# An attention and mixture-of-experts kernel: another set-up of the routing, the last head's low parts on VectorE, and the sum of query halves one head earlier

## The chip, the cores and the metric

The kernel runs on one core of a Trainium2 chip. The metric is the time of one execution on the device in microseconds (us): the median of several runs, lower is better.

## The reference

Attention with queries averaged in pairs, then a mixture of experts in which each token goes to the one expert with the largest logit.

```python
q_pool = q.reshape(B, H, S // 2, 2, D).mean(axis=3)          # B, H, S, D = 4, 8, 1152, 64
scores = 1 / np.sqrt(D) * np.matmul(q_pool, k.transpose(0, 1, 3, 2))
attn = np.exp(scores - scores.max(-1, keepdims=True))
attn = attn / (attn.sum(-1, keepdims=True) + 1e-09)
x = np.matmul(attn, v).transpose(0, 2, 1, 3).reshape(B * S // 2, H * D)   # 2304 x 512
xn = x / (np.linalg.norm(x, axis=-1, keepdims=True) + 1e-06)
en = expert_emb / (np.linalg.norm(expert_emb, axis=-1, keepdims=True) + 1e-06)
logits = xn @ en.T / tau                                     # 8 experts
expert_idx = np.argmax(logits, axis=1)
gate_w = softmax(logits)[np.arange(N), expert_idx]
out[mask] = gate_w[mask, None] * (np.maximum(x[mask] @ w1[e], 0.0) @ w2[e])   # per expert e
```

Everything is in float32; the kernel keeps the accuracy by splitting float32 values into a high and a low 16-bit part.

## The kernel before

**Attention.** There are 32 heads, written here as head 0 to head 31 (`g` in the code); two heads make a pair, four pairs a batch. The loop over `g` (line 1071 on) writes nine steps for each head, `c` = 0 to 8, one for each 128 keys. A step holds, in the order of the letters in `ORDER`: S, the scores of 128 keys by 576 queries on TensorE (line 309) and their exponential on ScalarE (line 311); M, matmuls for the row maxima of the next head (lines 260 and 266, then ScalarE 272 and VectorE 275, 277, 283); E, the low part of the exponentials of one step earlier, `EL = e - high(e)` (line 313); P, the product of the exponentials of the head before with the values (lines 389 to 391), which reads the low parts in line 391; X, everything else that a table puts at that step. Every engine runs its own instructions in the order in which this loop writes them.

The low part of a step is on GpSimd for the steps listed in `POOL_EL` (1, 2, 4, 5, 6, 7 in an even head, 0, 1, 3, 5, 8 in an odd one) and on VectorE for the others. `PVH` sets what P takes: in step 0 keys 0 to 3 of the first query tile, in step 1 keys 4 to 7, in step 2 key 8, then the other tiles. So TensorE comes to the low part of step 7 at the end of step 1 of the next head.

**Preparation of a pair.** `load_qk` reads queries and keys by the SP queue at step 2 of an even head (`LPOS`). `prep` gives seven operations that `QPOS` puts into the odd head that follows: `qsum`, the sum of the two query halves (GpSimd, line 174), at step 1, then high and low parts of keys and queries (ScalarE 177 and 186, GpSimd 180 and 189). The DMAs that move the parts are in the next even head.

**Set-up of the routing.** `setup_routing` (line 435) normalises the expert vectors: squares and their sum, a square root by three Newton iterations (`root_steps`), a reciprocal, high and low parts, two DMA transposes. It returns a list of steps, and from head 4 on the loop takes one after each step `c`.

**Routing of a batch.** `rsteps` splits the attention output, makes logits, and `chains` finds the expert and the rank of each token: `mx`, `lgs`, `mark`, `mk`, `choose` (one-hot `oh`), `rank` (matmuls), `rk`, `rq`, `rm`, and `oneh`, a comparison of 128 x 512 or 128 x 640 elements into `AV` (line 614). For batches 0 to 2 these run beside the attention of the next batch, also one step of the list after each step `c`; some are on GpSimd (`w`), some on VectorE.

**The end of attention.** In heads 30 and 31 the output of the last batch is split in three quarters of its columns (`split`, lines 485 to 494): high part on ScalarE, low part on VectorE (488), DMAs, and the sum of squares on VectorE (494). Iteration `g` = 32 holds only the P of head 31. Then the string `TAIL` gives the order in which normalising of head 31 (`N`, `J`), the last quarter (`c`, `R`), logits (`A`, `L`), expert choice, gathers and the first expert blocks are written, and `run` the other blocks: gather of 128 tokens (867), transpose (871), `mm1` (911), `relu` (917, 918), `mm2` (928), scaling (934), scatter (935). The expert weights are read as float32 and split by ScalarE (884) and VectorE (882).

Of the kernel before, what the change touches and what calls it, by code (L numbers as in the profile page):

```python
# [10 lines left out]
BF16 = mybir.dt.bfloat16  # L11
# [31 lines left out]
def attn_moe(ctx: ExitStack, tc: tile.TileContext, qt, kt, vt, emb, tau, w1, w2, out):  # L43
# [259 lines left out]
    def sc(g, c):  # L303
# [8 lines left out]
        eng = nc.gpsimd if c in (POOL_EL[g % 2] if g else POOL_E0) else nc.vector  # L312
# [18 lines left out]
    QPOS = [1, 2, 3, 3, 5, 7, 8]  # L331
# [12 lines left out]
    TAIL = 'x.0.0 x.0.1 A.0 A.1 A.2 A.3 mm1.0.0 j.4 N c.1.5.0 j.4 c.1.5.1 J c.0.1.0 j.2 c.0.1.1 R x.0.2 x.0.3 ch.1.2 ch.1.3 cl.1.0 cl.1.1 cl.1.2 cl.1.3 x.1.0 x.1.1 x.1.2 x.1.3 S A.4 mm1.0.1 mm1.1.0.0.6 L mm1.1.0.6.12 q.5 relu.0.0 q.2 mm1.1.1.0.4 q.5 mm1.1.1.4.12 mm2.0.0.6 q.11 relu.0.1 E relu.1.0 relu.1.1 g.24 gather.2 gather.3 gather.4 gather.5 xtr.2 xtr.3 xtr.4 regl.5 regl.6 wl.5.0 wl.5.1 mm2.0.6.24 mm2.1 mm1.2.0 g.2 mm1.2.1 fin.0 fin.1 cst.5.0.0 cst.5.0.1'  # L344
# [90 lines left out]
    def setup_routing():  # L435
# [23 lines left out]
        def turn():  # L459
# [24 lines left out]
    def split(T, x, xh, c0, c1, now, xt):  # L484
# [35 lines left out]
    def last_part(b):  # L520
# [715 lines left out]
```

## Time and profile before

| | |
|---|---|
| Time, median of 3 runs (lowest, highest) | 681.13 us (678.55, 682.29) |
| The profiled execution: its own time, its span | 676.58 us, 674.9 us |
| Busy share of TensorE, VectorE, ScalarE, GpSimd | 93%, 83%, 75%, 63% |
| Granted TensorE clock, mean | 0.99 |

The profile gives one execution on the chip. A share of busy time is a mean over stages: attention up to about 439 us and expert blocks after it. Below, a head is the stretch from its first exponential on ScalarE (line 311, nine in each head) to that of the next head. A `[... <-X]` behind a row is the idle time of that engine just before the instruction, and what ended it.

### The profile page before, as it was taken

Reading aid. Unit: us, or ns where it says so; the run is one execution under the profiler, and the core shown is the slowest. Engines: PE = TensorE matmul, PEld = TensorE weight load, DVE = VectorE, ACT = ScalarE, POOL = GpSimd, SP = SyncE. Lnnn points to the kernel's source line nnn. Section 1 sums busy time; section 2 is a strip of 40 time slices with the busy share of each in tenths; the row PEclk is TensorE's granted clock in tenths of the full one; section 3 lists DMA queues with packets and bytes.
Section 4 is the critical chain, followed back from the end, with each engine's and each line's share of the span. In section 5 each row is a group of like instructions: output and inputs, shape, how many; then the busy total and the mean of one; then the engine's idle time right before and its main releaser. Section 6 shows DMA issues by size and latency. Waiting matters only on the chain. (4 is left out here: it accounts for less than half of the span.)

```text
span 674.9 us, 22284 instructions
## 1 busy us (share of the span) xinstructions
PE 628.4 (93%) x8898; PEld 471.3 (70%) x8918; DVE 563.2 (83%) x983; ACT 509.4 (75%) x839; POOL 425.2 (63%) x349
## 2 busy tenths in 40 slices
PE   8999979999899799899899989799999999999994
PEld 2477757777678577678677768686776767768671
DVE  6778777888787978887878898996758999999996
ACT  2888767788887688897789867532548898988985
POOL 5699899897897887887996858202231233464231
PEclk9999998999999999999999999799999999999999
DMA  6844615537675529675529615996899977232881
GB/s 197 244 120 132 184 39 164 155 95 200 160 146 153 155 67 227 152 168 168 138 77 232 156 56 182 197 284 140 245 287 297 198 207 187 69 85 72 207 189 44
DMA packets 82990, 109.18 MB, mean 162 GB/s; under 512 B 51406, under 2 KB 57070, under 8 KB 82880
## 3 DMA queue, kind: packets, MB, share of 16 engines
q1 hardware_dynamic: 79280, 96.68, 55.7%
q0 software_dynamic: 3600, 11.01, 5.7%
q8 instruction: 72, 1.18, 0.7%
q14 instruction: 38, 0.31, 0.1%
HBM read 118.52 MB, written 10.22 MB: 191 GB/s over the span
## 5 line engine op out<-in xcount | busy, mean ns | idle before, releaser
L313 POOL TENSOR_TENSOR ar<-ar 128x576 f16<-128x576 f32 x175 | 222.4, 1278 | 56.9 <-ACT ar L311 56.2
L311 ACT ACTIVATE ar<-st 128x576 f32<-128x576 f32 x288 | 187.0, 652 | 63.0 <-PE st L309 59.0
L309 PE MATMUL st<-ar 128*128 128x288 f16 (+1 forms) x1152 | 188.6, 286 | 0.4 <-ACT ar L311 0.3
L882 DVE TENSOR_TENSOR ar<-ld,ar 128x1024 bf16<-128x1024 f32 x144 | 167.5, 1218 | 10.0 <-ACT ar L884 9.2
L391 PE MATMUL acc<-ar 128*128 128x65 f16 (+1 forms) x1440 | 166.9, 193 | 6.2 <-DVE ar L313 3.9
L389 PE MATMUL acc<-ar 128*128 128x65 f16 (+1 forms) x1440 | 167.8, 194 | 0.2
L390 PE MATMUL acc<-ar 128*128 128x64 f16 (+1 forms) x1440 | 167.7, 196 | 0.0
L389 PEld LDWEIGHTS <-ar 128*128 128x128 bf16 (+1 forms) x1440 | 136.3, 98 | 32.1 <-issue 19.7
L390 PEld LDWEIGHTS <-ar 128*128 128x128 bf16 (+1 forms) x1440 | 136.0, 98 | 22.9 <-issue 2.0
L884 ACT ACTIVATE ar<-ld 128x1024 f16<-128x1024 f32 x144 | 143.1, 1050 | 8.3 <-DMA ld<-in_w_dram 8.3
L275 DVE CUSTOM_DVE_ANT_0 my<-m,my 128x512 bf16<-128x512 f32 x139 | 95.6, 687 | 57.1 <-PE m L260 38.7
L391 PEld LDWEIGHTS <-ar 128*128 128x128 f16 (+1 forms) x1440 | 136.4, 100 | 8.0 <-DVE ar L313 4.4
L935 POOL DMA_INDIRECT out_dram<-ar,six x21 | 42.1, 2004 | 135.5 <-ACT ar L934 125.2
L313 DVE TENSOR_TENSOR ar<-ar 128x576 f16<-128x576 f32 x113 | 124.0, 1098 | 0.0
L911 PEld LDWEIGHTS <-ar 128*128 128x128 f16 (+1 forms) x2016 | 114.1, 98 | 5.4 <-issue 1.2
L911 PE MATMUL hps<-ar 128*128 128x128 f16 x2016 | 116.5, 219 | 0.9 <-DMA ar<-ar 0.9
L928 PE MATMUL ops<-ar 128*128 128x512 f16 (+1 forms) x484 | 111.2, 379 | 2.3 <-ACT ar L884 1.3
L309 PEld LDWEIGHTS <-ar 128*128 128x128 f16 (+1 forms) x1152 | 95.5, 98 | 21.6 <-issue 3.4
L928 PEld LDWEIGHTS <-ar 128*128 128x128 f16 x504 | 48.4, 98 | 56.2 <-ACT ar L884 1.7
L272 ACT ACTIVATE my<-m 128x512 bf16<-128x512 f32 x139 | 82.8, 595 | 2.4 <-PE m L260 2.3
L260 PE MATMUL m<-ld,qz 128*128 128x512 f16 (+1 forms) x264 | 62.8, 299 | 10.2 <-DVE mc L277 6.1
L260 PE MATMUL m<-kd,qz 128*128 128x512 f16 x132 | 50.2, 380 | 6.6 <-DVE mc L275 3.2
(212 smaller groups left out, 654.9 us busy)
## 6 DMA issues: line engine op xcount, KB each, us to landing
ld<-in_w_dram SPq DMA_DIRECT2D x160, 512.0 KB
ld<-in_q_dram SPq DMA_DIRECT2D x16, 576.0 KB
ld<-in_v_dram SPq DMA_DIRECT2D x16, 576.0 KB
ar<-ld SPq DMA_DIRECT2D x31, 288.0 KB
ld<-in_k_dram SPq DMA_DIRECT2D x15, 576.0 KB
ar<-ld SPq DMA_DIRECT2D x33, 144.0 KB
ar<-qhl SPq DMA_DIRECT2D x32, 144.0 KB
xs<-xh SPq DMA_DIRECT2D x13, 256.0 KB
```

The costliest lines, as they stand in the source:

```text
L260: nc.tensor.matmul(out=o, lhsT=QZ[s][:, c:c + 128], rhs=kr, start=True, stop=True)
L275: nc.vector.tensor_tensor_reduce(out=y, in0=m, in1=y, scale=1.0, scalar=-3e38, op0=ALU.add, op1=ALU.max, accum_out=mc[p, h][:, 1, t:t + 1])
L309: nc.tensor.matmul(out=st[:, a, 0:HQ], lhsT=KK[s][0:n, h, k, c * 128:(c + 1) * 128], rhs=QQ[s][0:n, h, k, a * HQ:(a + 1) * HQ], start=(k = ...
L311: nc.scalar.activation(out=e.rearrange("p (a q) -> p a q", a=2), in_=st[:, :, 0:HQ], func=AF.Exp, scale=1.0 / 16)
L313: return lambda: eng.tensor_tensor(out=EL[g % 2][:, c], in0=e, in1=hi(e), op=ALU.subtract)
L389: nc.tensor.matmul(out=a[r], lhsT=hi(e[:, w]), rhs=VV[s][:, c, h, 0:65], start=(x == 0), stop=False)
L390: nc.tensor.matmul(out=a[r, 0:64], lhsT=hi(e[:, w]), rhs=VV[s][:, c, h, 65:129], start=False, stop=False)
L391: nc.tensor.matmul(out=a[r], lhsT=el[:, w], rhs=VV[s][:, c, h, 0:65], start=False, stop=(x == NC - 1))
L882: nc.vector.tensor_tensor(out=dl.bitcast(BF16), in0=src, in1=dh, op=ALU.subtract)
L884: nc.scalar.activation(out=dh, in_=src, func=AF.Copy)
L911: nc.tensor.matmul(out=hp[j, f][:, t * 128:t * 128 + 128], lhsT=wv(w, i % 2, c)[:, u], rhs=xt[:, 2 * c + i // 2], start=(c == 0 and t == 0 ...
L928: nc.tensor.matmul(out=op[j], lhsT=ht[:, c // 4, i // 2, (c % 4) * 128:(c % 4) * 128 + 128], rhs=wv(w, i % 2, c), start=(k == 0), stop=(k ...
```

## The change

- **Set-up.** The squares of the expert vectors with their sum, the scaling by the reciprocal and the high part move to ScalarE. The product with 64 becomes an operation on the 16 x 1 reciprocal. The list grows from 22 steps to 42 with gaps: the Newton iterations stand in head 6 and not in heads 4 to 6, the rest in heads 6 to 8.
- **Last head.** For `g` = 31 all nine low parts are on VectorE. In `split` the sum of squares on VectorE goes; `first_squares` makes it on ScalarE, at `Q` in `TAIL`.
- **Query halves.** `qsum` for pair p + 2 leaves step 1 of the odd head and is written at step 7 (`QSUM`) of the even head before, the head whose step 2 issues the load that it reads.
- **Routing of a batch.** The lists of `rsteps` have empty steps put in and operations regrouped.

```diff
-        eng = nc.gpsimd if c in (POOL_EL[g % 2] if g else POOL_E0) else nc.vector
+        eng = nc.gpsimd if g < 2 * B * NP - 1 and c in (POOL_EL[g % 2] if g else POOL_E0) else nc.vector
...
-    QPOS = [1, 2, 3, 3, 5, 7, 8]
+    QSUM = 7
+    QPOS = [2, 3, 3, 5, 7, 8]
...
-    TAIL = 'x.0.0 x.0.1 A.0 A.1 A.2 A.3 mm1.0.0 j.4 N c.1.5.0 ...
+    TAIL = 'x.0.0 x.0.1 A.0 A.1 A.2 A.3 mm1.0.0 Q j.4 N c.1.5.0 ...
...
-        steps = [[loads], [masks], [iotas], []]
-        steps += [[f] for f in [
-            lambda: gp.tensor_scalar(out=taub, in0=taub, scalar1=XS * 64.0, scalar2=None, op0=ALU.mult),
-            lambda: gp.tensor_tensor(out=e2, in0=e, in1=e, op=ALU.mult),
-            lambda: v.tensor_reduce(out=sq, in_=e2, axis=AX.X, op=ALU.add),
-        ] + root + [
-            lambda: gp.tensor_scalar(out=r, in0=n, scalar1=1e-6, scalar2=None, op0=ALU.add),
-            lambda: v.reciprocal(out=r, in_=r),
-            lambda: gp.tensor_scalar(out=e2, in0=e, scalar1=r, scalar2=64.0, op0=ALU.mult, op1=ALU.mult),
-            lambda: gp.tensor_copy(out=eh[:, 0], in_=e2),
-            lambda: gp.tensor_tensor(out=eh[:, 1], in0=e2, in1=eh[:, 0], op=ALU.subtract),
-            turn,
-        ]]
+        def squared():
+            nc.scalar.activation(out=e2, in_=e, func=AF.Square, accum_out=sq)
+
+        parts = [
+            (0, loads), (1, masks), (2, iotas), (7, squared), (10, root[0]), (10, root[1]),
+            (30, lambda: gp.tensor_scalar(out=taub, in0=taub, scalar1=XS * 64.0, scalar2=None, op0=ALU.mult)),
+            (25, lambda: gp.tensor_scalar(out=r, in0=n, scalar1=1e-6, scalar2=None, op0=ALU.add)),
+            (28, lambda: v.reciprocal(out=r, in_=r)),
+            (34, lambda: gp.tensor_scalar(out=r, in0=r, scalar1=64.0, scalar2=None, op0=ALU.mult)),
+            (36, lambda: nc.scalar.activation(out=e2, in_=e, func=AF.Copy, scale=r)),
+            (37, lambda: nc.scalar.activation(out=eh[:, 0], in_=e2, func=AF.Copy)),
+            (39, lambda: gp.tensor_tensor(out=eh[:, 1], in0=e2, in1=eh[:, 0], op=ALU.subtract)),
+            (41, turn),
+        ]
+        steps = [[] for _ in range(42)]
+        for i, f in enumerate(root[2:]):
+            steps[18 + i].append(f)
+        for i, f in parts:
+            steps[i].append(f)
...
-        if now:
-            sv = work.tile([128, 384], BF16, tag="sv", name="sv", bufs=1)
-            v.tensor_tensor_reduce(out=sv[:, 0:(c1 - c0) * 128], in0=xc, in1=xc, scale=1.0, scalar=0.0, op0=ALU.mult, op1=ALU.add, accum_out=ssq[:, T:T + 1])
...
+        def first_squares():
+            for i in range(n):
+                nc.scalar.activation(out=sj[:, 128:512], in_=x[:, i, 0:384], func=AF.Square, accum_out=ssq[:, T0 + i:T0 + i + 1])
...
-            return steps + [[f] for f in crit[:5] + cnt + crit[5:] + oneh]
+            return steps + [[f] for f in crit[:3]] + [[], crit[3:4], crit[4:5], [], cnt[0:1], cnt[1:], [], crit[5:6], crit[6:7], crit[7:8], crit[8:10], crit[10:], [], oneh]
...
-                plist[p + 2] = prep(p + 2)
                 for pos, f in zip(QPOS, plist[p + 2][0]):
                     at(pos, f)
             if g % 2 == 0 and p + 2 < NPAIR:
                 at(LPOS, lambda p=p: load_qk(p + 2))
+                at(QSUM, lambda p=p: (plist.update({p + 2: prep(p + 2)}), plist[p + 2][0].pop(0)()))
```

GpSimd's instructions around the Newton iterations (423, 424 before; 424, 425 now), first before, from the end of head 4; `ar` is the exponentials' arena, `ld` the loaded keys.

```order
L313 TENSOR_TENSOR ar<-ar 128x576 x3
L423 TENSOR_TENSOR n_279<-n_278 16x1
L423 TENSOR_TENSOR n_279<-n_279,esq 16x1
L313 TENSOR_TENSOR ar<-ar 128x576
L174 TENSOR_TENSOR qs<-ld 128x576
L424 TENSOR_SCALAR n_279<-n_279 16x1
L424 TENSOR_TENSOR n_278<-n_279,n_278 16x1
L313 TENSOR_TENSOR ar<-ar 128x576
```

And now, from the end of head 4 too:

```order
L313 TENSOR_TENSOR ar<-ar 128x576 x4
L174 TENSOR_TENSOR qs<-ld 128x576
L313 TENSOR_TENSOR ar<-ar 128x576 x3
L180 TENSOR_TENSOR ld<-ld 128x576
L313 TENSOR_TENSOR ar<-ar 128x576 x2
L189 TENSOR_TENSOR qhl<-qs,qhl 128x576
L180 TENSOR_TENSOR ld<-ld 128x576
L313 TENSOR_TENSOR ar<-ar 128x576
L424 TENSOR_TENSOR n_279<-n_278 16x1
L424 TENSOR_TENSOR n_279<-n_279,esq 16x1
```

The first iteration has left head 5, where the operations of `prep` stand, for the start of head 6, and `qs` stands in front of two low parts that it stood behind: step 7 of the even head and step 0 of the odd one.

VectorE in head 16, with the routing of batch 0, before:

```order
L313 TENSOR_TENSOR ar<-ar 128x576
L402 TENSOR_SCALAR r<-acc 128x5
L403 RECIPROCAL r<-r 128x5
L405 TENSOR_TENSOR xx<-acc,r 128x4x64
L407 TENSOR_SCALAR xx<-acc,r 64x64
L614 TENSOR_TENSOR av<-iota,rm 128x512
L275 ISA my,mc<-m,my 128x512
L275 ISA mc 128x1
L224 SCALAR_TENSOR_TENSOR ar<-ld,ar 128x18x64
```

And now:

```order
L403 TENSOR_SCALAR r<-acc 128x5
L404 RECIPROCAL r<-r 128x5
L406 TENSOR_TENSOR xx<-acc,r 128x4x64
L408 TENSOR_SCALAR xx<-acc,r 64x64
L275 ISA my,mc<-m,my 128x512
L275 ISA mc 128x1
L224 SCALAR_TENSOR_TENSOR ar<-ld,ar 128x18x64
L622 TENSOR_TENSOR av<-iota,rm 128x512
L275 ISA my,mc<-m,my 128x512
```

The comparison `av` has gone from in front of a maximum (275) to behind it and behind the values' low part (224).

VectorE in head 31, before (488 is the low half of the split, 494 the squares):

```order
L407 TENSOR_SCALAR xx<-acc,r 64x64
L488 SCALAR_TENSOR_TENSOR xh<-xx,xh 128x3x128
L494 ISA sv,ssq<-xx 128x384
L494 ISA ssq 128x1
L488 SCALAR_TENSOR_TENSOR xh<-xx,xh 128x3x128
L494 ISA sv,ssq<-xx 128x384
L494 ISA ssq 128x1
L313 TENSOR_TENSOR ar<-ar 128x576
L488 SCALAR_TENSOR_TENSOR xh<-xx,xh 128x3x128
```

And now:

```order
L408 TENSOR_SCALAR xx<-acc,r 64x64
L313 TENSOR_TENSOR ar<-ar 128x576
L495 SCALAR_TENSOR_TENSOR xh<-xx,xh 128x3x128
L313 TENSOR_TENSOR ar<-ar 128x576
L495 SCALAR_TENSOR_TENSOR xh<-xx,xh 128x3x128
L313 TENSOR_TENSOR ar<-ar 128x576 x2
L495 SCALAR_TENSOR_TENSOR xh<-xx,xh 128x3x128
L313 TENSOR_TENSOR ar<-ar 128x576 x2
```

The squares are gone from VectorE and five low parts have come in between.

## Rows read from the trace of the kernel before

**Rows 1.** Windows, heads 3 to 6: from:to length, busy us by engine, PEclk, DMA.

```profile
56.16:68.78 12.62, 12.25 (x194) 9.37 (x193) 10.34 (x22) 10.54 (x20) 11.95 (x9) 1.00 0.28 73
68.78:79.93 11.15, 11.15 (x189) 9.02 (x188) 7.83 (x19) 9.31 (x17) 7.86 (x14) 1.00 0.80 220
79.93:94.61 14.68, 12.46 (x194) 9.47 (x193) 12.24 (x25) 10.54 (x19) 14.11 (x21) 1.00 0.17 54
94.61:110.99 16.38, 13.04 (x189) 9.95 (x188) 10.44 (x19) 9.52 (x18) 15.76 (x16) 0.90 0.56 154
```

**Rows 2.** Waits, 79 to 106 us: who waited for whom, total us, times, longest.

```profile
DVE er L470 <- POOL er L469: 3.7, 1, 3.7
...
PE acc L391 <- POOL ar L313: 2.3, 2, 1.7
```

**Rows 3.** Waits of TensorE in heads 15 and 16, 211 to 239 us.

```profile
PE mt L293 <- DVE mc L275: 1.9, 1, 1.9
...
PE m L260 <- DVE mc L275: 1.7, 1, 1.7
```

**Rows 4.** Waits, 425 to 440 us.

```profile
ACT ar L531 <- DVE xx L405: 6.5, 1, 6.5
...
PE acc L391 <- DVE ar L313: 3.9, 4, 2.0
```

**Rows 5.** Windows: a stretch in the P of head 31, columns as in Rows 1.

```profile
429.40:436.23 6.83, 5.27 (x68) 3.86 (x65) 6.69 (x15) 4.06 (x5) 0.00 (x0) 0.50 1.20 204
```

**Rows 6.** Groups on GpSimd: count, then busy us, mean ns, idle before.

```profile
L313 POOL TENSOR_TENSOR ar<-ar 128x576 f16<-128x576 f32 x175 | 222.4, 1278 | 56.9 <-ACT ar L311 56.2
...
L174 POOL TENSOR_TENSOR qs<-ld 128x576 f32<-128x576 f32 x15 | 27.8, 1852 | 2.7 <-DMA ld<-in_q_dram 2.7
...
L423 POOL TENSOR_TENSOR n<-n 16x1 f32<-16x1 f32 x3 | 2.1, 697 | 0.0
...
L423 POOL TENSOR_TENSOR n<-n,esq 16x1 f32<-16x1 f32 x3 | 0.5, 180 | 0.2
```

**Rows 7.** Windows of heads 8 and 12, columns as in Rows 1.

```profile
123.60:135.07 11.47, 11.24 (x189) 9.01 (x188) 9.47 (x18) 9.32 (x17) 8.80 (x8) 1.00 0.76 208
...
173.99:186.08 12.09, 11.33 (x188) 9.02 (x187) 8.50 (x19) 10.24 (x20) 8.76 (x7) 1.00 0.79 184
```

**Rows 8.** Timeline of TensorE in head 9: start, us, then the instruction.

```profile
136.91 0.65 PE L309 MATMUL st<-ar 128*128 128x288 f16 x4
```

**Rows 9.** Timeline: a query load and its sum, then head 8, then a load in head 12.

```profile
10.57 0.58 SPq L137 DMA_DIRECT2D ld<-in_q_dram  x1
...
14.87 1.40 POOL L174 TENSOR_TENSOR qs<-ld 128x576 f32<-128x576 f32 x1 [2.65 <-DMA ld<-in_q_dram]
...
128.72 0.61 SPq L137 DMA_DIRECT2D ld<-in_q_dram  x1
...
131.76 1.15 POOL L313 TENSOR_TENSOR ar<-ar 128x576 f16<-128x576 f32 x1 [0.39 <-ACT ar L311]
...
181.00 0.60 SPq L137 DMA_DIRECT2D ld<-in_q_dram  x1
```

**Rows 10.** Timeline of VectorE in heads 15 and 16: two operations of the routing.

```profile
218.36 0.19 DVE L605 TENSOR_REDUCE mk<-key 128x4 f32<-128x32 f32 x1 [0.80 <-POOL key L587]
...
233.53 1.56 DVE L614 TENSOR_TENSOR av<-iota,rm 128x512 f16<-128x512 f32 x1
```

**Rows 11.** Timeline of VectorE, 419 to 438 us.

```profile
419.69 2.19 DVE L488 SCALAR_TENSOR_TENSOR xh<-xx,xh 128x384 f16<-128x384 f32 x1 [0.59 <-ACT xh L487]
...
422.28 3.14 DVE L488 SCALAR_TENSOR_TENSOR xh<-xx,xh 128x384 f16<-128x384 f32 x1
...
425.82 0.75 DVE L313 TENSOR_TENSOR ar<-ar 128x576 f16<-128x576 f32 x1
...
426.49 1.50 DVE L488 SCALAR_TENSOR_TENSOR xh<-xx,xh 128x384 f16<-128x384 f32 x1
...
429.06 0.54 DVE L488 SCALAR_TENSOR_TENSOR xh<-xx,xh 128x384 f16<-128x384 f32 x1
```

More of the change, by code (lines that the diff above doesn't have):

```diff
@@ L343, in attn_moe @@
     C00 = [18, 19, 20, 21]
-    TAIL = 'x.0.0 x.0.1 A.0 A.1 A.2 A.3 mm1.0.0 j.4 N c.1.5.0 j.4 c.1.5.1 J c.0.1.0 j.2 c.0.1.1 R x.0.2 x.0.3 ch.1.2 ch.1.3 cl.1.0 cl.1.1 cl.1.2 cl.1.3 x.1.0 x.1.1 x.1.2 x.1.3 S A.4 mm1.0.1 mm1.1.0.0.6 L mm1.1.0.6.12 q.5 relu.0.0 q.2 mm1.1.1.0.4 q.5 mm1.1.1.4.12 mm2.0.0.6 q.11 relu.0.1 E relu.1.0 relu.1.1 g.24 gather.2 gather.3 gather.4 gather.5 xtr.2 xtr.3 xtr.4 regl.5 regl.6 wl.5.0 wl.5.1 mm2.0.6.24 mm2.1 mm1.2.0 g.2 mm1.2.1 fin.0 fin.1 cst.5.0.0 cst.5.0.1'
+    TAIL = 'x.0.0 x.0.1 A.0 A.1 A.2 A.3 mm1.0.0 Q j.4 N c.1.5.0 j.4 c.1.5.1 J c.0.1.0 j.2 c.0.1.1 R x.0.2 x.0.3 ch.1.2 ch.1.3 cl.1.0 cl.1.1 cl.1.2 cl.1.3 x.1.0 x.1.1 x.1.2 x.1.3 S A.4 mm1.0.1 mm1.1.0.0.6 L mm1.1.0.6.12 q.5 relu.0.0 q.2 mm1.1.1.0.4 q.5 mm1.1.1.4.12 mm2.0.0.6 q.11 relu.0.1 E relu.1.0 relu.1.1 g.24 gather.2 gather.3 gather.4 gather.5 xtr.2 xtr.3 xtr.4 regl.5 regl.6 wl.5.0 wl.5.1 mm2.0.6.24 mm2.1 mm1.2.0 g.2 mm1.2.1 fin.0 fin.1 cst.5.0.0 cst.5.0.1'
     RC = 1
@@ L547, in logit @@
                 lmm(L[:, i * NE:(i + 1) * NE], xbt, 3, 4, 2 * i, first=False, last=(i == n - 1))
-        return cut, rest, squares, add_up, logit
+        return cut, rest, first_squares, squares, add_up, logit
     def chains(b, last):
@@ L690, in rsteps @@
         if not late_:
-            return steps + [[f] for f in crit[:5] + cnt + crit[5:] + oneh]
+            return steps + [[f] for f in crit[:3]] + [[], crit[3:4], crit[4:5], [], cnt[0:1], cnt[1:], [], crit[5:6], crit[6:7], crit[7:8], crit[8:10], crit[10:], [], oneh]
         sel, pick, nxt = early_steps()
-        steps += [crit[0:2], crit[2:4], [crit[4], cnt[0]], cnt[1:], [], crit[5:6], sel[0:1], crit[6:8], crit[8:10] + sel[1:2], [crit[10], sel[2]]]
-        steps += [sel[3:5], sel[5:7], sel[7:9], oneh, pick[0:2], pick[2:5], pick[5:6], pick[6:7], [], pick[7:8], [], pick[8:10], pick[10:11], pick[11:13], nxt]
+        steps += [crit[0:3], [], crit[3:5], [], cnt, crit[5:6], sel[0:1], crit[6:8], crit[8:10] + sel[1:2], [crit[10], sel[2]]]
+        steps += [sel[3:5], sel[5:7], sel[7:9], pick[0:2], pick[2:5], oneh, pick[5:6], pick[6:7], [], pick[7:8], [], pick[8:10], pick[10:11], pick[11:13], nxt]
         return steps
@@ L1168, in attn_moe @@
         ended.append(True)
-        cut, rest, squares, add_up, logit = last_part(B - 1)
+        cut, rest, first_squares, squares, add_up, logit = last_part(B - 1)
         L = small("L")
@@ L1183, in attn_moe @@
             "R": rest,
-            "S": squares,
+            "S": squares, "Q": first_squares,
             "A": lambda i: fl[i](L),
```

## The prediction

> **What bounds the kernel now.** I read the windows of the heads first, because a mean over 675 us hides which head is long. An even head without routing takes 11.15 us, and TensorE is busy for all of it; an odd one takes 12.62 us, with TensorE busy for 12.25 (head 3 in [rows 1]). So TensorE sets the time where nothing disturbs it, and only waits of TensorE, or its clock, can be won back. Heads 5 and 6, with the set-up, take 14.68 and 16.38 us, 2.06 and 5.23 more than the undisturbed 12.62 and 11.15: 7.3 us together. GpSimd is busy for 14.11 and 15.76 of these [rows 1], nearly without a pause, so there it is the bound. The waits show how that reaches TensorE: it waits for low parts of GpSimd, and VectorE stands 3.7 us at the reciprocal behind GpSimd, with the maxima queued behind it [rows 2]. In heads 15 and 16 TensorE waits 1.9 and 1.7 us for VectorE's maxima [rows 3]. At the end of attention it waits 3.9 us for low parts of VectorE [rows 4], and the granted clock is 0.50 of full, the lower of its two levels (1.2 and 2.4 GHz), for 6.83 us from 429.40 on, where TensorE had just stood waiting [rows 5].
>
> **The sum's base.** The profiled execution has a span of 674.9 us and took 676.58, 4.55 under the median of 681.13. I work the gains out from its rows and take them off the median.
>
> **Set-up.** Three operations of GpSimd on 16 x 512 elements go (squares, scaling, copy). By the nearest row, 1.28 us for a low part of 128 x 576 [rows 6], that is at most 3.8 us; the small operation that comes in costs at most 0.70. The larger part is that the Newton iterations leave head 5, where GpSimd also has keys and queries to split. I follow GpSimd's queue through head 6 as it is now written. Without the set-up head 5 takes 12.6 us, so head 6 begins at 79.93 + 12.6 = 92.5. The last low part of head 5 comes at the earliest 1 us later, 93.5. Then there are 13 small operations in five groups: the first of a group took 0.70, a following one 0.18 [rows 6], with gaps of about 0.1 that makes 5 x 0.70 + 8 x 0.18 + 0.4 = 5.3. Six low parts at 1.15 (128 x 576 undelayed, [rows 9]) are 6.9, the query sum 1.40 [rows 9]. The low part of step 7 is so done at 93.5 + 5.3 + 6.9 + 1.4 = 107.1. TensorE comes to it 1.84 us after the next head begins: in head 9 the third group of scores starts at 136.91, right behind that product, and the head began at 135.07 [rows 7, 8]. Head 7 would begin at 92.5 + 11.15 = 103.65, so TensorE is there at 105.5 and waits 1.6 us. Of 7.3 us there remain about 2 with the wait at the reciprocal: **-5.4**. Bounds: GpSimd at its mean of 1.28 a low part and 1.85 for the sum [rows 6] adds 1.2, and heads 4, 7 and 8 can each lose some 0.5, so -2.5; nothing left, -7.3. What ScalarE takes over is four instructions of under 0.7 us in heads in which it is busy for 9.3 to 10.5 of 11.2 to 12.6 us [rows 1], so they are hidden.
>
> **Query sum.** GpSimd does the same work, earlier. No row shows TensorE waiting for GpSimd in an undisturbed odd head, so nothing is won there. The new order puts the sum in front of the low part of step 7, and in front of both stands the query load. From its issue to the sum it took 14.87 - 10.57 = 4.3 us. In head 8 the load is issued at 128.72, so it is there at 133.0; the low part of step 6 ends at 132.9 [rows 9]. Then the sum to 134.4 or 134.9, the low part to 135.6 or 136.2, and TensorE needs it at 136.9: hidden, with 0.7 to 1.3 us to spare. In head 12, where routing DMAs stand before the load in SP's queue, it is issued at 181.00 [rows 9], 7.0 us after the head's start instead of 5.1 [rows 7]: there at 185.3, sum and low part done at 188.4, while TensorE is there at 186.08 + 1.84 = 187.9. It waits 0.5 us, or 1.5 if the busier queue costs the load 1 us more. Head 20 is of the same kind. I take **+1.3** for the 13 odd heads, between 0 and 4 (a third of a microsecond in each).
>
> **Routing of a batch.** In head 15 VectorE stood 0.80 us for GpSimd's key with a maximum queued behind; in head 16 the comparison `av` of 1.56 us stood before the maximum for which TensorE waited 1.7 [rows 3, 10]. The first now asks after the normalising, some 1.5 us later, when the key is done; the second now stands behind the maximum and the values' low part. That is 0.8 + 1.5 for batch 0. For batch 1, where the same pattern occurs with shorter waits, I count 1.2, for batch 2 nothing: **-3.5**. Bounds: 0, if `av` only delays the next maximum; -7.2, if both waits vanish in both batches.
>
> **Last head.** VectorE loses five sums of squares, about as long as the low halves of equal shape (0.54): 2.7 us. Three of its five low halves took 2.19, 3.14 and 1.50 against 0.54 for the others [rows 11]; beside the three GpSimd was at low parts, and it will be idle: 5.2 us. It gains five low parts at 0.75: 3.7. So it is through 2.7 + 5.2 - 3.7 = 4.2 us earlier, and what follows (normalising, weight parts, normalising of head 31) is its own queue. TensorE's 3.9 us of waits shrink by about as much, and at the higher clock it has some 2 us more in hand. The squares now lie on ScalarE, which stood 6.5 us before it could cut the last quarter [rows 4]; five of about 0.65 (0.54 and the reading of the sum) are 3.3 us and fit, and would cost 3.3 if that pause closed. **-4.2**. Bounds: -2, if the clock falls again and GpSimd's gathers slow VectorE; -6 with the clock held.
>
> **Sum.** -5.4 + 1.3 - 3.5 - 4.2 = -11.8: 681.1 - 11.8 = **669.3 us**, about 669.
>
> **Rivals.**
> (1) *Part of it.* GpSimd is the bound in head 6 for longer and the clock still falls: set-up -3, last head -2, routing -1.5, query sum +1.3, together -5.2: **676**. For it speaks that in head 6 GpSimd has 15 us of work for 11; against it, that head 7 has the room.
> (2) *The expert blocks give the last term back*, since the weights come no earlier: -11.8 + 4.2: **673.5**. Against it: the loads wait for numbers that are worked out behind this same chain.
> (3) *The waits only move*: behind the moved operations the next maximum is as late, and set-up saves only what it removes. Then -2.5 (set-up) - 4.2 + 1.3 + 2 for the set-up's new place in heads 7 and 8, -3.4: **678**, at the edge of no change.
> (4) *Slower: the query sum is held.* Beside each other the two engines slow down: a low half of VectorE took 3.14 instead of 0.54 us [rows 11]. The Trainium skill (SBUF — State Buffer, Who interferes with whom) says that a VectorE instruction with two SBUF inputs and a GpSimd one that reads SBUF exclude each other for the whole instruction, and that the order of issue decides who waits; by that rule the sum, now beside the values' low part on VectorE, is held or holds. The stretch in the row agrees with it. Held by the 2.6 us of that row, the low part of step 7 is 1.3 to 1.9 us too late in each of 13 odd heads, 17 to 25 us, less 13.1 of the other terms: **685 to 693**. It decides from a hold of about 2 us (0.7 to 1.3 to spare and 13.1 / 13 = 1.0). Against it: the odd heads are freed of the same neighbours.
>
> **How the numbers follow.** Forecast 0.55, (1) 0.21, (2) 0.10, (3) 0.08, (4) 0.06. Half a per cent, 3.4 us, is about what a measurement of this kernel can tell from no change. Faster: 0.55 + 0.21 + 0.10 = 0.86; same 0.08; slower 0.06. The range goes from 662 (the larger ends of two terms) to 678, which takes in (1) and (2) and the edge of (3).
>
> **What would show it.** Heads 5 and 6 near 12.6 and 11.2 to 13 us, a wait of TensorE for GpSimd's low part near the start of head 7, no wait of the reciprocal over 1 us. Low halves (495) of 0.54 in head 31, waits of TensorE for VectorE's low parts near 1 us, full clock around 430, the cast of the weights (890) some 4 us earlier. Head 16 near 11.5 to 12 us. A wait at the query sum for its load in heads 12 and 20 alone. It would be wrong if odd heads without routing became longer than 12.6 us, or if waits of TensorE for maxima came back behind `av`.

## The result

The changed kernel takes 674.67 us (median of 4 runs, 668.95 to 676.48) beside 681.71 for the kernel before (4 runs): ratio 0.9899, 95% interval 0.9862 to 0.9936, so 7.0 us or 1.0% faster. A second comparison, of 6 runs beside 23, gave 671.99 beside 679.64, ratio 0.9884 (0.9845 to 0.9924). 669 was forecast, from a gain of 12 us; 59% of that gain came in the first comparison and 67% in the second (7.9 us on 680). The profiled execution of the changed kernel took 675.21 us, with a span of 673.5. Two executions, one of e4 and one of e5 below, count as slow and are left out of those two ratios, but not of the medians printed with them.

First the heads with the set-up, 4 to 8 in this view of windows (from:to and length, busy us of TensorE, weight loads, VectorE, ScalarE and GpSimd, then granted clock, DMA share, GB/s):

```profile
68.62:80.95 12.33, 11.31 (x189) 9.01 (x188) 9.05 (x19) 10.02 (x20) 9.17 (x15) 1.00 0.77 197
80.95:93.33 12.38, 11.85 (x194) 9.32 (x193) 10.74 (x24) 10.53 (x19) 12.30 (x9) 1.00 0.26 74
93.33:105.00 11.67, 11.32 (x189) 9.02 (x188) 8.24 (x18) 9.45 (x18) 11.01 (x20) 1.00 0.76 205
105.00:118.79 13.79, 12.02 (x194) 9.37 (x193) 11.08 (x23) 10.53 (x19) 13.62 (x13) 1.00 0.24 66
118.79:131.73 12.94, 11.65 (x188) 9.07 (x187) 11.35 (x19) 10.26 (x19) 10.44 (x9) 1.00 0.66 182
```

Heads 5 and 6 are at 12.38 and 11.67, where [rows 1] had 14.68 and 16.38, and the clock is full. But head 4 is 12.33 where it was 11.15, head 7 is 13.79 (the odd head without disturbance took 12.62), head 8 is 12.94 where [rows 7] had 11.47. TensorE's waits between 104 and 132 us say who is late there (before, none in this window was over 0.2):

```profile
PE acc L392 <- POOL ar L313: 1.2, 1, 1.2
PE m L260 <- DVE mc L275: 0.9, 1, 0.9
```

The routing's heads 15 and 16: TensorE's waits [rows 3] of 1.9 and 1.7 have become 1.1 and none, and head 16 has shrunk from 13.32 to 11.26. Head 17, which follows, has grown from 12.63 to 13.96, and GpSimd is busy in all of it. First the wait that is left in heads 15 and 16, then the windows of heads 16 and 17:

```profile
PE mt L293 <- DVE mc L275: 1.1, 1, 1.1
```

```profile
220.77:232.03 11.26, 11.26 (x193) 9.12 (x192) 9.71 (x23) 9.36 (x17) 9.87 (x12) 1.00 0.86 221
232.03:245.99 13.96, 11.98 (x194) 9.38 (x193) 11.21 (x23) 10.54 (x19) 13.96 (x10) 1.00 0.23 65
```

Head 25 shows how GpSimd gets late: the timeline of GpSimd has the query sum 1.20 us idle before its load, the low parts behind it, then TensorE's wait for one of them, and right behind that a stretch at half clock (1.2 GHz). Timeline, waits and window in that order:

```profile
335.17 1.40 POOL L174 TENSOR_TENSOR qs<-ld 128x576 f32<-128x576 f32 x1 [1.20 <-DMA ld<-in_q_dram]
336.52 3.88 POOL L313 TENSOR_TENSOR ar<-ar 128x576 f16<-128x576 f32 x3
```

```profile
PE acc L392 <- POOL ar L313: 2.0, 1, 2.0
```

```profile
339.70:342.60 2.90, 2.90 (x34) 2.45 (x33) 2.45 (x4) 2.32 (x4) 2.90 (x3) 0.50 0.01 3
660.60:663.40 2.80, 2.80 (x8) 1.06 (x7) 2.80 (x3) 2.80 (x4) 1.50 (x1) 0.50 0.23 85
429.40:436.23 6.83, 5.92 (x135) 5.62 (x134) 6.28 (x20) 5.25 (x14) 0.00 (x0) 1.00 0.70 158
441.80:445.10 3.30, 3.29 (x46) 3.27 (x47) 1.59 (x6) 0.60 (x1) 0.00 (x0) 0.50 1.04 322
```

The third of these windows answers [rows 5]: where the clock was 0.50 it is 1.00. The fourth shows that a fall has come back 12 us later, behind a wait that is new (below). Up to there the end of attention is as forecast. TensorE waits 1.0 for VectorE's low parts instead of 3.9, ScalarE 1.5 before it cuts the last quarter instead of 6.5 [rows 4], and VectorE's five low halves (now line 495) take 0.55 each [rows 11]:

```profile
PE L L505 <- DMA ar<-ar: 2.1, 1, 2.1
PE acc L392 <- DVE ar L313: 1.0, 1, 1.0
PE L L505 <- DMA xt<-xh: 0.9, 1, 0.9
```

```profile
L495 DVE SCALAR_TENSOR_TENSOR xh<-xx,xh x5: 549/551/559, 417.3 to 424.5; 128x384 f16<-128x384 f32 x5
```

The first expert block begins 7.1 us earlier than before (432.65 against 439.74). But the first two rows above are new: TensorE, early now, waits 2.1 + 0.9 us for the transposed copies on which the logits depend, and the clock falls there. And at the other end it waits for the casts of the last block's weights, by the timeline of TensorE; before, there was one such wait of 1.27:

```profile
657.17 0.38 PE L936 MATMUL ops<-ar 128*128 128x512 f16 x1 [1.08 <-ACT ar L892]
659.16 6.81 PE L936 MATMUL ops<-ar 128*128 128x512 bf16 x23 [1.61 <-DVE ar L890]
```

Behind that the clock falls again (660.60 above), and 23 matmuls take 6.81 us instead of 5.34. From the 193rd matmul of the first layers to the last, TensorE runs 4.2 us ahead of the kernel before, in lock step; at its last matmul 0.9 of it are left. So this one pair of traces differs by 1.4 us only, while the medians differ by 7; the runs had to say why.

### The profile page after: what moved, and what is told of

Same layout as the page of the kernel before. It is cut to its first block, busy times and chain, and to the rows that moved or that the text cites. A ratio compares the mean times of both kernels' runs of the same rounds, so it can differ in the third digit from the quotient of the medians.

```text
span 673.5 us, 22297 instructions
## 1 busy us (share of the span) xinstructions
PE 627.0 (93%) x8918; PEld 471.3 (70%) x8918; DVE 549.8 (82%) x977; ACT 513.5 (76%) x853; POOL 419.0 (62%) x342
## 5 line engine op out<-in xcount | busy, mean ns | idle before, releaser
L313 POOL TENSOR_TENSOR ar<-ar 128x576 f16<-128x576 f32 x170 | 225.6, 1339 | 38.4 <-ACT ar L311 36.2
L313 DVE TENSOR_TENSOR ar<-ar 128x576 f16<-128x576 f32 x118 | 126.8, 1077 | 0.0
L943 POOL DMA_INDIRECT out_dram<-ar,six x21 | 36.1, 1720 | 142.3 <-ACT ar L942 132.9
L936 PE MATMUL ops<-ar 128*128 128x512 f16 (+1 forms) x504 | 114.0, 383 | 2.7 <-DVE ar L890 1.6
L875 POOL DMA_INDIRECT ar<-xs,gix x24 | 34.4, 1432 | 40.4 <-DMA ld<-in_w_dram 33.5
```

The costliest lines, as they stand in the source:

```text
L313: return lambda: eng.tensor_tensor(out=EL[g % 2][:, c], in0=e, in1=hi(e), op=ALU.subtract)
L936: nc.tensor.matmul(out=op[j], lhsT=ht[:, c // 4, i // 2, (c % 4) * 128:(c % 4) * 128 + 128], rhs=wv(w, i % 2, c), start=(k == 0), stop=(k ...
```

## The experiments

All ratios are to the kernel before on the same chip; us are worked out on 680.

**A second look at both kernels.** No edit; first the changed kernel.

e1, expected:

> The changed kernel once more, next to the three below on one chip. It is here for a second trace: in the first one the matmuls waited 7.3 us for GpSimd's low parts behind the heads in which the query sum is now made, and the granted clock fell twice, at 339.7 and at 660.6. Theory 1 (these waits belong to the order of the work): the same heads, 7, 13, 17, 21 and 25, show the same waits of 0.9 to 2.2 us. Theory 2 (they are chance of one execution, from a late transfer): other heads or none. Time by both near 674.7, ratio near 0.990.

671.99 us, ratio 0.9884 (0.9845 to 0.9924). The order of the work explains the waits: heads 7, 13 and 17 have them again at 1.2 to 1.3 us, head 25 at 1.3 (2.0 in the first trace), with no fall of the clock there; head 21 is without. So theory 1, but the size of a wait and the clock behind it differ from one execution to the next.

e8, expected:

> The kernel before once more, for a second trace of it: the first came from an execution of 676.58, three us under the median of 679.6, with a mean granted clock of 0.990 where the median of its executions has 0.985. Theory 1: the difference is half clock behind waits of the matmuls that the first trace shows at full clock (heads 15, 16, 23 or 29) or longer stretches behind those in head 6 and at 429. Theory 2: transfers that land later, so other and longer waits at the same clock.

This execution of the kernel before took 682.73 us, 6 more than the first. Its heads 0 to 5 are the same to 0.03 us, and head 6, where both have a fall of the clock, takes 17.66 instead of 16.38. Then there are falls behind waits which the first trace has at full clock, in heads 15, 23 and 29. Windows of the first two (13.99 and 13.80 in the first trace, clock 1.00):

```profile
212.25:227.70 15.45, 13.55 (x198) 10.36 (x197) 12.28 (x26) 10.65 (x20) 14.41 (x14) 0.89 0.24 68
316.62:331.43 14.81, 13.16 (x198) 10.25 (x197) 11.24 (x26) 10.55 (x20) 13.91 (x14) 0.92 0.19 55
```

Theory 1: the waits are the same in both traces (1.9, 1.7 and 1.9 us for VectorE's maxima), the clock is at its lower level for some 3 us after each, and each head is 1.0 to 1.5 us longer (head 29: 15.65 instead of 14.23). At the start of head 31 this execution is 4.6 of its 6 us behind. That is the usual case: the median of the mean granted clock is 0.985 over 23 executions of the kernel before and 0.992 over the 6 of the changed one. (1 - 0.985) x 2 x 677.9 = 20.3 us at the lower level, against 10.7; half of the difference, 4.8 us of the 7.9, is an estimate from above of what the clock accounts for: it also counts stretches in which TensorE has nothing left to do, as behind the last matmul of e8, where the clock is at 0.50 from 677.1 us on.

**Each part alone on the kernel before.** The set-up:

```
+        parts = [(0, loads), (1, masks), (2, iotas), (7, squared), ...,
+            (30, lambda: gp.tensor_scalar(out=taub, in0=taub, ...)), ...]
```

e4, expected:

> The kernel before with the new set-up alone. Theory 1 (the prediction): heads 5 and 6 fall from 14.68 and 16.38 to about 12.6 and 11.2, heads 7 and 8 pay at most 1.6 of it back, 5.4 us faster, 676.3, ratio 0.992. Theory 2 (the waits only move): heads 4, 7 and 8 pay back 4 us or more, as they did in the first trace of the changed kernel (together 3.9 us longer), so at most 3 us faster, ratio 0.9955 or above. If heads 7 and 8 stay at 12.62 and 11.47 here, their loss in the changed kernel is the query sum's.

679.36 us, ratio 0.9973 (0.9939 to 1.0008). Heads 5 and 6 win all of their 7.3 us (12.62 and 11.16), and heads 4, 7 and 8 give 6.2 of it back (11.15, 12.62 and 11.47 before):

```profile
68.73:81.44 12.71, 11.32 (x189) 9.02 (x188) 10.37 (x19) 10.02 (x20) 9.58 (x15) 1.00 0.70 191
...
105.22:118.83 13.61, 12.19 (x194) 9.38 (x193) 9.74 (x23) 10.54 (x20) 13.45 (x12) 1.00 0.16 49
118.83:133.97 15.14, 13.03 (x188) 10.19 (x187) 11.62 (x19) 10.26 (x19) 11.04 (x10) 0.89 0.60 165
```

Theory 2, and the loss of heads 7 and 8 is the set-up's, not the query sum's. Head 7 is the wait for GpSimd that the prediction worked out (1.6 forecast, 1.0 here). Heads 4 and 8 it did not have. In the timelines of head 4, first VectorE and GpSimd of the kernel before, then of this one:

```profile
74.70 0.76 DVE L313 TENSOR_TENSOR ar<-ar 128x576 f16<-128x576 f32 x1
```

```profile
76.66 0.26 POOL L465 TENSOR_SCALAR taub<-taub 128x1 f32<-128x1 f32 x1 [2.12 <-DMA taub<-in_tau_dram]
```

```profile
74.66 2.67 DVE L313 TENSOR_TENSOR ar<-ar 128x576 f16<-128x576 f32 x1
```

```profile
73.35 6.21 POOL L313 TENSOR_TENSOR ar<-ar 128x576 f16<-128x576 f32 x5
```

Before, GpSimd stood 2.12 us for the load of tau, and VectorE's low part beside that pause took 0.76. The new set-up scales tau much later; GpSimd runs five low parts without a pause, and the same instruction of VectorE takes 2.67. The next maximum is as much later and TensorE waits 1.4 for it. In head 8 a low part of VectorE takes 3.30 beside GpSimd instructions that follow each other, TensorE waits 1.7, and the clock falls (0.89 above).

The one operation that made the pause was then put back in its place (on the kernel with the query sum put back, whose heads 4 to 8 are those of the set-up alone):

```
-            (30, lambda: gp.tensor_scalar(out=taub, in0=taub, ...)),
+            (4, lambda: gp.tensor_scalar(out=taub, in0=taub, ...)),
```

e11, expected:

> The kernel with the sum put back (e2) and one operation of the new set-up, GpSimd's scaling of tau, back at its old step 4, where it waits about 2 us for its load. Theory 1 (VectorE's low part in head 4 takes 2.67 us instead of 0.76 because GpSimd works beside it without a pause): GpSimd pauses 2.1 us before 77, VectorE's low part at 74.7 is back at 0.76, the matmuls' wait of 1.55 for maxima is gone and head 4 is back at 11.15; head 5 or 6 pays at most 1 us for GpSimd's later low parts. Theory 2 (VectorE is late for another reason of the new set-up): the low part and head 4 stay as in e2. The time as e2's within 1.5 us by either.

669.45 us, ratio 0.9822 (0.9777 to 0.9866). Theory 1, by timelines of both engines and the window of head 4:

```profile
74.79 0.75 DVE L313 TENSOR_TENSOR ar<-ar 128x576 f16<-128x576 f32 x1
```

```profile
77.10 1.37 POOL L468 TENSOR_SCALAR taub<-taub 128x1 f32<-128x1 f32 x1 [2.47 <-DMA taub<-in_tau_dram]
```

```profile
68.87:80.02 11.15, 11.15 (x189) 9.01 (x188) 7.83 (x19) 9.84 (x19) 7.51 (x14) 1.00 0.80 210
80.02:94.08 14.06, 12.33 (x194) 9.44 (x193) 10.23 (x24) 10.54 (x21) 14.06 (x11) 1.00 0.20 65
119.39:131.66 12.27, 11.57 (x188) 9.09 (x187) 10.40 (x18) 10.14 (x19) 11.45 (x9) 1.00 0.74 204
```

A wait on GpSimd was worth 1.5 us to VectorE and TensorE in its head. GpSimd's later low parts cost 1.4 in head 5 and 0.5 in head 6 (forecast: at most 1), so heads 4 to 6 together gain nothing (36.9 us, 36.5 without the pause). Over heads 4 to 8 it is 62.8 us instead of 65.1, all of it from head 8 (12.27 instead of 15.0), where VectorE's low part takes 1.98 instead of 3.30 and the clock does not fall. The ratio is not told apart from that of the same kernel without the pause (0.9842, e2 below).

The routing's step lists alone:

```
-        steps += [crit[0:2], crit[2:4], [crit[4], cnt[0]], cnt[1:], [], ...]
+        steps += [crit[0:3], [], crit[3:5], [], cnt, crit[5:6], ...]
```

e5, expected:

> The kernel before with the routing's new step lists alone. Theory 1 (the prediction): 3.5 us faster by the shorter waits for maxima in heads 15, 16, 23 and 24, 676.1, ratio 0.995. Theory 2 (the parts add up): what the parts done alone leave over of the 10.7 us by which the changed kernel with its query sum put back beats the kernel before, that is 8.8 us, 670.8, ratio 0.987, since the matmuls' wait of about 2 us in head 15 is, in most executions, followed by some us at half clock (as behind the same wait in the trace with the new set-up alone), which goes with the wait. Theory 3: neither, ratio above 0.998, and the parts don't add up.

677.2 us, ratio 0.9931 (0.9905 to 0.9957): 4.7 us. Windows of heads 15 and 16 (13.99 and 13.32 in the first trace of before):

```profile
212.63:225.24 12.61, 12.08 (x194) 9.36 (x193) 11.88 (x25) 10.54 (x19) 11.71 (x12) 1.00 0.20 62
225.24:237.46 12.22, 11.44 (x193) 9.18 (x192) 10.55 (x23) 9.47 (x17) 10.89 (x13) 1.00 0.78 204
```

Heads 23 and 24 are at 12.63 and 12.30 (13.80 and 12.69). That is 4.0 us less at full clock in the four, and against the second trace of before another 1.9, since with the waits their falls of the clock are gone too. Between theories 1 and 2; the mechanism of theory 2 is there, its 8.8 us are outside the interval (2.9 to 6.5).

The move of the query sum alone:

```
+                at(QSUM, lambda p=p: (plist.update({p + 2: prep(p + 2)}), plist[p + 2][0].pop(0)()))
```

e6, expected:

> The kernel before with the move of the query sum alone. Theory 1 (the prediction): 1.3 us slower, 680.9, ratio 1.002. Theory 2 (the difference of the changed kernel with and without it): 3 us slower, 682.6, ratio 1.004, with waits of the matmuls for GpSimd's low parts of 0.9 to 1.5 us in heads 13, 17, 21 and 25. Theory 3 (it trades waits between a pair's heads): the odd heads lose as in theory 2, but heads 16 and 24 gain 1 us each and heads 7 and 8 are shorter than without it, in all within 1 us of before.

679.85 us, ratio 0.9986 (0.9958 to 1.0013), 1.0 us faster with zero inside: theory 3 comes nearest by the time, but not by its mechanism, for heads 16 and 24 gain nothing (13.33 and 12.70). Undisturbed odd heads take 12.39 instead of 12.62, head 10 12.16 instead of 12.61; head 13 takes 14.29, with a wait of 1.7 for GpSimd, instead of 12.62, and head 27 14.51 instead of 13.83. Heads 17 and 25 stay at 12.62 and 12.38: the move alone does not make them wait.

The last head alone:

```
+        eng = nc.gpsimd if g < 2 * B * NP - 1 and c in (...) else nc.vector
```

with the five squares on ScalarE.

e3, expected:

> The kernel before with the last head's part of the change alone: five low parts from GpSimd to VectorE, the first squares from VectorE to ScalarE. Theory 1 (the prediction): 4.2 us faster, 677.5, ratio 0.994; the full clock around 430 and the matmuls' waits for VectorE's low parts down from 4.1 to 1. Theory 2 (the expert blocks give it back): the head ends as much earlier, but the logits wait for the transposed copies (about 3 us) and the last matmuls wait for the weight casts (1.6 us more), so 0 to 2 us faster, ratio 0.997 to 1.000.

679.56 us, ratio 0.9995 (0.997 to 1.002; 12 runs): theory 2. The waits of TensorE from 418 to 447 us in this kernel are those of the changed one:

```profile
PE L L498 <- DMA ar<-ar: 2.0, 1, 2.0
```

**The changed kernel without one part.** Without the last head's part:

e7, expected:

> The changed kernel with the last head as before (five low parts on GpSimd, first squares on VectorE). Theory 1 (the prediction): 4.2 us slower than the changed kernel, 676, ratio 0.9945. Theory 2 (what the last head gains goes into the wait of the last block's matmuls for the weight casts, as for the kernel before with that part alone, which measured 0.1 us): the same time as the changed kernel, 672, ratio 0.988 to 0.990; the expert blocks begin 3 us later and their last matmuls wait 3 us less.

673.23 us, ratio 0.9888 (0.9852 to 0.9924), that of the changed kernel: theory 2. The second-layer products begin 4.3 us later than in the second trace of the changed kernel (1.6 of it by a fall of the clock in heads 29 and 30), and yet the last matmul starts 0.5 us earlier. The last two waits of TensorE in both, e7 first:

```profile
657.34 5.34 PE L935 MATMUL ops<-ar 128*128 128x512 f16 x24 [1.08 <-ACT ar L891]
```

```profile
654.39 0.38 PE L936 MATMUL ops<-ar 128*128 128x512 f16 x1 [2.36 <-ACT ar L892]
656.38 6.79 PE L936 MATMUL ops<-ar 128*128 128x512 bf16 x23 [1.61 <-DVE ar L890]
```

What stood in front of the late weights in the changed kernel: ScalarE's casts waited for the weight loads, and these stood on SyncE's queue behind a transposing copy. First SyncE's queue and ScalarE's wait for loads in that trace (e1), then in that of the last experiment below (e12), where TensorE waited only 0.9 us at the end:

```profile
637.03 5.73 SPq L879 DMA_TRANSPOSE ar<-ar  x1
```

```profile
ACT ar L892 <- DMA ld<-in_w_dram: 3.8, 3, 1.8
```

```profile
633.45 2.93 SPq L879 DMA_TRANSPOSE ar<-ar  x1
```

```profile
ACT ar L892 <- DMA ld<-in_w_dram: 0.8, 1, 0.8
```

The same views give 2.8 us for that copy in the first trace of before, with last waits of 1.3; 3.5 and 2.7 in the first of the changed kernel; 4.6 and 3.7 with the sum put back. In the other traces the link is looser: 3.8 us in e3 went with a last wait of 1.1. From the start of head 31 to the end of the last matmul it is 248.9 to 250.1 us in six traces without the last head's part; with it 244.6 to 247.3 in five and 250.9 to 251.8 in three, which are the three with the long last waits (2.7 to 4.0 us; at most 1.9 in the others). So the part does win 1.6 to 5.5 us, and loses them and a little more where the weights come late. That its median gain is nothing suggests that this is the usual case, which no trace counts (the trace of the part alone, with 246.5, is from the shortest of its 12 executions). What makes the weights late in one execution and not in another stays open.

The trace of this kernel (e7) shows a second thing. From the end of its last matmul to the end of the kernel it took 12.2 us, where the changed kernel took 7.0. GpSimd's next to last output scatter lies beside a run of eight casts on VectorE (timelines of GpSimd and VectorE, e7, then e1):

```profile
658.79 7.48 POOL L942 DMA_INDIRECT out_dram<-ar,six  x1 [5.05 <-DVE ar L889]
```

```profile
656.24 9.16 DVE L889 TENSOR_TENSOR ar<-ld,ar 128x1024 bf16<-128x1024 f32 x8
```

```profile
657.97 1.50 POOL L943 DMA_INDIRECT out_dram<-ar,six  x1 [6.68 <-ACT ar L942]
```

```profile
655.12 9.16 DVE L890 TENSOR_TENSOR ar<-ld,ar 128x1024 bf16<-128x1024 f32 x8
```

It took 7.48 us, until 0.9 after VectorE's run ended, or 1.50. In ten traces it took 7.3 to 7.5 in three, where it began 2.5 to 2.7 us after the casts, and 1.2 to 1.5 in seven, where it began 2.85 to 3.2 after them. Four of the eight casts were for a block that doesn't exist, so they can go behind the branch:

```
+            if f in (cast, wl) and a[0] == 1 and j >= lim[f] - 1 and j > EB + 1:
+                return
```

e10, expected:

> The changed kernel, in which the second-layer weights of a block that may not exist are cast after the branch that decides on it and no longer ahead of it (here that block doesn't exist: four of VectorE's last eight casts served nothing). Theory 1 (VectorE's unbroken run of casts holds GpSimd's next to last output scatter in some executions: 7.3 to 7.5 us instead of 1.2 to 1.5 in three of ten traces, and 12.3 us instead of 7 to 9 from the last matmul to the end): VectorE's last run is 4 casts long, no scatter takes over 4.5 us, the time from the last matmul to the end is at most 8 us, the median 1 to 2 us under the changed kernel's and the spread of its executions narrower. Theory 2 (the slow scatters have another cause): 12 us tails go on and the median stays.

672.17 us, ratio 0.9878 (0.9836 to 0.9919). Timelines of GpSimd and VectorE:

```profile
658.86 2.99 POOL L943 DMA_INDIRECT out_dram<-ar,six  x1 [5.00 <-DVE ar L890]
```

```profile
656.36 4.62 DVE L890 TENSOR_TENSOR ar<-ld,ar 128x1024 bf16<-128x1024 f32 x4
```

The scatter began 2.5 us after the casts, as in the held ones, and took 2.99, again until 0.9 after VectorE's run, now half as long, had ended: it is the run of casts that holds it. From the last matmul to the end it took 7.5. The median did not move against the changed kernel, neither of whose two traces has a hold: theory 1 is right on the cause, and its weight in that kernel was overrated.

With the query sum back in the second head:

```
-    QPOS = [2, 3, 3, 5, 7, 8]
+    QPOS = [1, 2, 3, 3, 5, 7, 8]
```

e2, expected:

> The changed kernel with one part undone: the sum of the next queries' halves stands again at step 1 of the pair's second head. Theory 1 (the prediction): the move costs 1.3 us, so this kernel takes 673.4, ratio near 0.988. Theory 2 (the trace of the changed kernel): the move costs 5 to 7 us, because the sum waits for its load at step 7 and GpSimd's low parts, for which the matmuls of the next head wait, stand behind it; this kernel takes 668 to 670, ratio 0.980 to 0.983, its heads 13, 17, 21 and 25 are back at 12.6 and the wait of the matmuls for GpSimd's low parts falls from 6.5 us to under 2.

668.69 us, ratio 0.9842 (0.9793 to 0.9892), 2.9 us under the changed kernel, but the two intervals overlap. The time is that of theory 2, the gain about half of its 5 to 7 us. Heads 13, 17, 21 and 25 are back at 12.6, 12.4, 12.5 and 12.8 (13.7, 14.0, 12.9 and 14.3 in the second trace of the changed kernel), and heads 16 and 24 pay 1.0 to 1.2 (12.45 and 12.30 instead of 11.26 and 11.31). So I tried both, by pairs:

```
+                if g < QLAST:
+                    at(QSUM, lambda p=p: ...)   # QLAST = 12
```

e9, expected:

> The changed kernel with the query sum in the pair's first head up to head 10 only, and at step 1 of the second head from there on. Theory 1 (the move pays in the set-up's heads, 4 to 11, and costs from head 12 on, as the traces with and without it show head by head: 2.6 us gained there, 3.5 us lost here): heads 13, 17, 21 and 25 at 12.4 to 12.8 and none of the matmuls' waits for GpSimd's low parts over 1.3 us, head 31 begins at 408.5 to 409.5 instead of 412.3, and about half of that is left at the end: 669 to 670.5, ratio 0.984 to 0.986. Theory 2 (the move is neutral, as alone on the kernel before, ratio 0.9986): the time of the changed kernel, 672 to 673.

668.49 us, ratio 0.9814 (0.9767 to 0.9861), the lowest of all. Heads 13 to 29 are as expected; head 31 begins at 410.7 and not at 409, because in this execution head 7 took 16.31 us. Head 6 was 0.5 us shorter than in the changed kernel, TensorE so came earlier to GpSimd's low part, waited 2.1 us for it instead of 1.2, and the clock fell. e10, whose attention is that of the changed kernel, shows the same (11.16 and 16.31), so this is a difference between executions. Against the changed kernel's 0.9884 that is 0.0070, with the two half widths taken together (root of 0.0040 and 0.0047 squared) 0.0062: faster than the changed kernel by a little more than its uncertainty, as the lowest of several variants and measured on another chip, so hardly shown.

Last, what makes the query sum late: its load, or GpSimd's own work?

```
+            if g and g % 2 == 0 and p + 2 < NPAIR:
+                at(0, lambda p=p: load_qk(p + 2))      # ahead of the pair's copies
```

e12, expected:

> The changed kernel with the loads of the pair after next at the start of a pair's first head, ahead of the 12 copies on SyncE's queue that stood before them (only SyncE's order differs). Theory 1 (the query sum costs what it does in heads 13, 21 and 25 because it waits for its load at step 7, and the low parts for the next head stand behind it): the loads land 4 to 8 us earlier, the sum's waits of 1.2 to 1.9 us in heads 4, 12, 20 and 24 are gone, the matmuls' waits for GpSimd's low parts in heads 13, 21 and 25 (1.34, and in one trace each 1.3 and 1.5 to 2.2) are under 0.4, head 17, where the sum didn't wait, keeps its 1.5; 2 to 3 us faster than the changed kernel, 669.5, ratio 0.984. Theory 2 (it is GpSimd's own work of 1.4 to 2.5 us that is late there, load or no load): the waits in 13 and 25 stay over 0.9 and the time at 672. Theory 3: the 12 copies, now 1.3 us and more later, become late for the matmuls or the maxima (waits for copies of the queries in odd heads), 674 or more.

671.8 us, ratio 0.9836 (0.98 to 0.9872): the ratio is that of theory 1, but 0.0048 from the changed kernel's, where the two half widths together are 0.0054. Both theories, head by head. The waits of GpSimd in head 12 and of TensorE in head 13, e1, then e12, which has no such row of GpSimd:

```profile
POOL qs L174 <- DMA ld<-in_q_dram: 2.3, 1, 2.3
```

```profile
PE acc L392 <- POOL ar L313: 1.2, 1, 1.2
PE mt L293 <- DVE mc L275: 0.6, 1, 0.6
```

```profile
PE mt L293 <- DVE mc L275: 0.7, 1, 0.7
```

Head 13 is at 12.54 instead of 13.74: theory 1. Heads 17 and 25 keep their waits of 1.3 (13.97 and 14.31, as in e1): theory 2. In the heads before them, 16 and 24, GpSimd has the routing's operations as well, and these heads are 1.4 to 2.1 us shorter than in the kernel before.

## Why the prediction came out as it did

| part | forecast, us | alone, ratio (95%) | us |
|---|---|---|---|
| set-up | -5.4 (-2.5 to -7.3) | 0.9973 (0.9939 to 1.0008) | -1.8 |
| query sum | +1.3 (0 to +4) | 0.9986 (0.9958 to 1.0013) | -1.0 |
| routing | -3.5 (0 to -7.2) | 0.9931 (0.9905 to 0.9957) | -4.7 |
| last head | -4.2 (-2 to -6) | 0.9995 (0.997 to 1.002) | -0.3 |
| all | -11.8 | 0.9884 (0.9845 to 0.9924) | -7.9 |

Direction and range held, but not for the reason that the whole sum gave. Of the four terms only the routing came out inside its own bounds, the others outside them, with intervals that reach in. Set-up and last head won 7.5 us less than forecast, and 3.5 of that came back by query sum and routing, which did better than forecast; that the errors went both ways is luck. The 674.67 of the first comparison lies between rival 1 (676) and rival 2 (673.5).

The parts alone add up to -7.8, with an uncertainty of 3.9 us (the four half widths taken together), so this agrees with -7.9 without being a close test; the plain medians give the set-up 0.3 and the routing 3.7. And the parts act on each other: the query sum won 1.0 alone and cost 2.9 on top of the other three (e2), neither clear of its uncertainty.

**Set-up**, right in its mechanism. Heads 5 and 6 came to 12.4 and 11.7, the reciprocal's wait of 3.7 is gone, and TensorE waits at the start of head 7 for 1.0 to 1.2 us (1.6 forecast): walking GpSimd's queue through head 6 held. What failed is the sentence that heads 4, 7 and 8 "can each lose some 0.5": they lost 1.5, 1.0 and 3.7 in the trace with the set-up alone, of which head 7 was already in the forecast's 2 us. I costed GpSimd's lost pauses at nothing, although the trace of before showed GpSimd idle in head 4 (7.86 of 11.15 us in [rows 1]) with VectorE's low parts short beside it. For this term rival 3, the waits only move, was the right one.

**Routing**, right in place, sign and size. Four heads fell by 4.0 us at full clock: heads 15 and 16 by 2.5, where 2.3 was forecast, heads 23 and 24 by 1.6, where 1.2 was. The rest fits with the trace of before, which came from an execution 4.5 us under the median, in which the waits of 1.7 to 1.9 us were not followed by a fall of the clock; working out gains from that trace and taking them off the median left this out.

**Query sum.** The bound below nothing was missing: the clean odd heads won up to 0.23 us each, since the sum no longer stands in front of their low parts, while I wrote that nothing was to be won there. The wait at the load was forecast for heads 12 and 20 alone; it showed in 4, 12 and 20, and in 24 in the first trace. And the prediction's sign of being wrong came up: heads 13, 17 and 25 took 13.3 to 16.6 us, longer than 12.6. In 17 and 25 neither edit does it alone: they take 12.44 and 12.79 us with the routing alone (e5), 12.62 and 12.38 with the move alone (e6), and 13.97 and 14.31 with both (e1). Heads 16 and 24, 1.1 and 0.4 us shorter by the routing and no shorter by the move, are 2.1 and 1.4 shorter with both. GpSimd does not get through as early: the query sum written at step 7 of head 16 starts at 231.9 us in the first trace, 0.2 before head 17. I had added the terms as if each kept its cover. Rival 4, the sum held through all odd heads, was wrong: the waits stand in three to five heads, not 13.

**Last head.** In the first trace what the prediction named happened: low halves of 0.55, 1.0 us of TensorE's wait, full clock around 430, the first cast of weights 6.6 us earlier (433.6 to 426.9; 2.5 of it from the head's earlier start). But the full clock did not last. The logits waited for their transposed copies, 3.0 us here and 1.1 to 3.0 in the eight traces with this part, and the clock fell there, at 441.7 us in this trace and at 431.1 in e1, for some 3 us each. The forecast had neither. The waits for the last block's casts took the rest where they were long. That is rival 2, to which I gave 0.10; my argument against it, that the loads wait for numbers worked out behind the same chain, holds for the first loads and not for the last ones, which stand on SyncE's queue behind a transposing copy.

## What to carry to other kernels

A pause of one engine can be what keeps its neighbour fast: before a wait on GpSimd is taken away, look at what VectorE does beside it, and cost that at the stretched duration; a pause put back has its price too, here 1.5 us won in one head and about 2 lost in the next two. Terms of a sum share their cover; where one edit shortens a stretch, work out anew what was hidden in it. And a single trace of the kernel before is one draw: compare its granted clock with that of the other executions before its waits are priced.

## What the runs showed of the hardware

- A low part of VectorE on 128 x 576 takes 0.75 us alone and took 2.67 and 3.30 beside GpSimd instructions that followed each other with no gap over 0.24. The Trainium skill (SBUF — State Buffer, Who interferes with whom) says that a VectorE instruction with two inputs in SBUF and a GpSimd one that reads SBUF contend for a port that only one of them holds at a time. The traces agree, and show that VectorE can lose more than one turn: 2.67 - 0.75 = 1.9 us is more than one GpSimd low part of 1.24 (five in 6.21).
- The other way round, a run of eight VectorE casts (1.14 us apart) held one scatter of GpSimd for 7.3 to 7.5 us where it began 2.5 to 2.7 after the run's start, and let it through in 1.2 to 1.5 where it began 2.85 to 3.2 after it. Why the start matters stays open.
- Falls of the granted clock to 0.50 stood behind single waits of TensorE (1.5 us in head 29 of e7, 1.7 in head 8 of e4, 2.0 in head 25 of the changed kernel) or two smaller ones close together (1.2 and 0.6 in head 5 of e5), in some executions and not in others of the same kernel: behind the 1.9 us in head 15 in the second trace of before, not in the first. The length of the wait alone does not tell which: the 1.75 us in head 11 had no fall behind it in either trace of before.
